# Routing the second of four token batches one step sooner, and re-laying the last attention step, in a fused attention and mixture-of-experts kernel

## The chip, the cores and the metric

The kernel runs on one core of a Trainium2 chip. The metric is the device time of one execution in microseconds. A program is executed several times; the median of the runs shown is compared, and one further execution is recorded by the hardware profiler. TensorE (PE) multiplies matrices, VectorE (DVE) and ScalarE (ACT) work on rows of 128 partitions, GpSimd (POOL) does small arithmetic and issues gathers and scatters, and SyncE (SP) issues the plain transfers. Each engine runs its own list of instructions in order, and the lists wait for each other through semaphores.

## The reference

Attention with a local window of 96 keys and 8 global keys over 4 batches of 768 tokens and 8 heads, then a mixture of 8 experts in which every token goes to the one expert with the largest logit:

```python
scores = scale * q @ k.T + bias            # masked to 8 global and 96 local keys
a = softmax(scores);  x = (a @ v)          # 3072 tokens x 512
logits = x @ w_gate + modality_bias[modality_id]
e_idx = np.argmax(logits, axis=1)
gate_w = softmax(logits)[np.arange(N), e_idx]
for e in range(E):
    mask = e_idx == e
    h = np.maximum(x[mask] @ w1[e], 0.0)
    out[mask] = gate_w[mask, None] * (h @ w2[e])
```

## The kernel before

**Attention.** The 3072 tokens are 24 blocks of 128, six to a batch. `step(n)` for n = 0 to 24 is a software pipeline. In step n PE computes the scores of block n (`s_mm`, tiles `s`), DVE adds the bias and finds the maxima (`red`, tiles `sc` and `nmx`), ACT takes the exponentials (`pr`). For block n-1 PE turns the exponentials (`t_mm`, tiles `pt`), and DVE or ACT copies them out (`t_cp`, tiles `pT`: of the three, the first by DVE, two by ACT). For block n-2 PE multiplies with the values (`pv`, tiles `x`), DVE divides (`rinv`, `xr`) and turns the rows for the gate (`xt`), and SP writes them to `x_rows` in DRAM. Step 24 has no block of its own: it finishes blocks 22 and 23.

**Routing.** Two steps after a batch is complete its logits are made (`gate_b`, `gate_c`: steps 8, 14, 20 for batches 0, 1, 2). The functions `route_m` (DVE finds the maximum `mx`, POOL makes `dl` and `cand`), `route_o` (DVE reduces `cand` to `cm`, POOL makes the one-hot `oh`), `route_e`, `route_b` (PE counts with a triangular matrix into `pk`, DVE copies it to `pks`, POOL adds up `base` and `pos`), `route_d`, `route_f` and `route_c` (POOL scatters a row for each token into `ids_sorted`) are put behind later steps by `at(step, function, ...)`; `after(n)` runs them at the end of step n. `route_o` is called inside the step, between `rinv` and `xr`, through the table `mids`.

**The first experts.** From the counts of batches 0 and 1 POOL makes a plan (`plan_parts`, four pieces, tiles `uei`, `uoi`, `inv`): two slots `e0` and `e1` of 512 tokens of one expert each. SP loads the weights of `e0` (`ld_first`, tile `raw`) and the token lists (`ld_lists`, tile `ui`; for `e1` also `ld_q`, tile `uq`), POOL gathers the rows of `e0` (`gather_x`, tile `xg`, four pieces of 128 rows), PE turns them (`x_pe`, tiles `mt`), ACT and DVE split them into a rounded part `xh` and a remainder `xl` (`x_lo`). The weights are split likewise (`split`, `split_lo`: `ah` and `al`). Then the slots run: `l1` (first product, tile `ph`, then `hh` by ACT and `hl` by DVE) and `l2` (second product, tile `po`), 512-column matmuls from there to the end.

**What sets the order.** PE, ACT and DVE run in the order in which the code is written. The order of POOL and SP is chosen by a scheduler from the same program. PSUM has eight banks: `p_p` has two (`pt`), `p_x` two (`x`, later `ph`), `p_t` four (`s`, `mt` and others); a tile waits until the last reader of the bank's former tile is done.

Of the kernel before, what the change touches and what calls it, by code (L numbers as in the profile page):

```python
# [9 lines left out]
F32 = mybir.dt.float32  # L10
F32R = mybir.dt.float32r
# [58 lines left out]
def moe_attention_kernel(  # L70
# [16 lines left out]
    def p_t(name):  # L87
        return psum.tile([P, 512], F32, tag="pR", name=name, bufs=4)
# [342 lines left out]
    def gate_c(b):  # L431
        lgts[b] = gp.tile([P, NB, E], F32, tag="lgt", name=f"lgt{b}")
        lps = gt.pop(b)
        lq = p_t(f"lq{b}")
        for u in range(NB // 2):
            nc.tensor.matmul(
                lq[:, 2 * E * u : 2 * E * u + 2 * E], lps[:, u * P : (u + 1) * P], sel, start=True, stop=True
            )
        V.tensor_add(
            lgts[b],  # L440
            lq[:, 0 : NB * E].rearrange("p (t e) -> p t e", e=E),
            tbias[:, b * NB : (b + 1) * NB, :],
        )
# [72 lines left out]
    def route_b(b):  # L516


        oh = rt.pop(b)
        pk = (p_t if b + 1 < B else p_p)(f"pk{b}")  # L520
        ohf = oh.rearrange("p a e -> p (a e)")
        nc.tensor.matmul(pk[:, 0 : NB * E], tri, ohf, start=True, stop=True)
        nc.tensor.matmul(pk[:, NB * E : 2 * NB * E], ones, ohf, start=True, stop=True)
        pks = gp.tile([P, 2 * NB * E], F32, tag="pks", name=f"pks{b}", bufs=1)
        V.tensor_copy(pks, pk[:, 0 : 2 * NB * E])
        eng = nc.gpsimd if b + 1 < B else V
        for j in range(NB):
            eng.tensor_add(base[:, b, j + 1, :], base[:, b, j, :], pks[:, (NB + j) * E : (NB + j + 1) * E])
        if b + 1 < B:
            eng.tensor_copy(base[:, b + 1, 0, :], base[:, b, NB, :])  # L530
        pos = t3(b, "pos")
        eng.tensor_tensor(pos, pks[:, 0 : NB * E].rearrange("p (a e) -> p a e", e=E), base[:, b, 0:NB, :], ALU.add)
        eng.tensor_tensor(pos, pos, bm(ebase, NB), ALU.add)
        eng.tensor_tensor(pos, pos, oh, ALU.mult)
        rt[b, "pos"] = pos
# [141 lines left out]
    def ld_q(s):  # L677
        n = P * s.nt
        so = nc.sync.value_load(s.o_src, min_val=0, max_val=E * NT)
        s.uq = idq.tile([P, 4, 4, IDW], I32, tag="uq", name=f"uq{s.name}")  # L680
        src = ids[ds(so, n), :].rearrange("(g i t) o -> i g (t o)", g=4, t=s.nt)
        for b in range(4):
            nc.sync.dma_start(
                s.uq[M * b : M * b + M].rearrange("p g t o -> p g (t o)")[:, :, 0 : s.nt * IDW], src
            )
# [101 lines left out]
    def x_lo(s, t):  # L787
        sl = slice(t * P, (t + 1) * P)
        V.tensor_tensor(s.xl[:, :, sl], s.xf.pop(t), s.xh[:, :, sl].bitcast(F32), ALU.subtract)
# [7 lines left out]
        return s.hi[which, h, c // 2], s.lo[which, h, c // 2], c % 2 * 512  # L797

    def l1(s, g, bank=p_x):

        ph = bank(f"ph{s.name}{g}")
        nt = s.nt
        hh = mp.tile([P, 512], F32R, tag="hh", name=f"hh{s.name}{g}", bufs=3)
        hl = mp.tile([P, 512], F32R, tag="hl", name=f"hl{s.name}{g}", bufs=3)
        s.h[g] = hh, hl
        if nt == 1:
            for c in range(4):
                hi, lo, o = both(s, "a", g, c)
                xh, xl = s.xh[:, c, 0:P], s.xl[:, c, 0:P]
                nc.tensor.matmul(ph, xh, hi[:, o : o + 512], start=(c == 0), stop=False)  # L810
                nc.tensor.matmul(ph, xh, lo[:, o : o + 512], start=False, stop=False)
                pe_end[0] = nc.tensor.matmul(ph, xl, hi[:, o : o + 512], start=False, stop=(c == 3))
            s.ph = ph
            s.hr = mp.tile([P, 512], F32, tag="hr", name=f"hr{s.name}{g}")
            last[0] = nc.scalar.activation(s.hr, ph, AF.Relu)
            return
        n, k = P * nt, 4 // nt
        for i in range(k):
            f = k * g + i
            fs = f % 4 * P  # L820
            for c in range(4):
                hi, lo, o = both(s, "a", f // 4, c)
                hi, lo = hi[:, o + fs : o + fs + P], lo[:, o + fs : o + fs + P]
                xh, xl = s.xh[:, c, 0:n], s.xl[:, c, 0:n]
                out_ = ph[:, i * n : (i + 1) * n]
                nc.tensor.matmul(out_, hi, xh, start=(c == 0), stop=False)  # L826
                nc.tensor.matmul(out_, hi, xl, start=False, stop=False)  # L827
                pe_end[0] = nc.tensor.matmul(out_, lo, xh, start=False, stop=(c == 3))  # L828
        last[0] = nc.scalar.activation(hh, ph, AF.Relu)  # L829
        V.scalar_tensor_tensor(hl, ph, 0.0, hh.bitcast(F32), ALU.max, ALU.subtract)  # L830

# [311 lines left out]
    def at(n, f, *args):  # L1143
        todo.setdefault(n, []).append((f, args))
# [139 lines left out]

    LAST = NBLK - NB
    for b in range(B):
        n0 = b * NB
        eng = nc.gpsimd if b + 1 < B else V
        at(n0 + NB + 3, route_m if b + 1 < B else route_a, b)
        if b + 1 < B:  # L1290
            mids[n0 + NB + 4] = b
        at(n0 + NB + 4, route_e, b)
        at(n0 + NB + 4, route_b, b)
        at(n0 + NB + 5, route_d, b, eng)
        if b + 1 < B:
            at(n0 + NB + 6, route_f, b)
        if b + 2 == B:
            for g in range(4):
                at(n0 + NB + 6, lambda g=g: gather_q(eslots[1], 0, g, pt_end))
        for j in range(NB):  # L1300
            at(n0 + NB + 6 + (j, j // 3, j // 2, j // 2)[b], write_in_step, b, j)
# [73 lines left out]
            next(plan_e, None)  # L1375

    for j in range(4):
        at(LAST - 1 + j, plan_part)

    def pool(name, bufs=1):  # L1380
        return sM.enter_context(tc.tile_pool(name=name, bufs=bufs, side="right", reuse_waits="tile"))
# [17 lines left out]
    def ld_lists():  # L1399
        with tc.issue_after(v_last[0].ins):  # L1400
            for s in eslots:
                lists[0] = ld_x(s)
                if not s.rows:
                    ld_q(s)


    def first_lo(j, h):
        fs = slice(512 * h, 512 * h + 512)
# [7 lines left out]
    at(LAST + 1, open_moe)  # L1416
    for j in range(2):
        at(LAST + 3, ld_first, "a", j)
    at(LAST + 4, ld_lists)
    at(LAST + 4, lambda: load_v(NBLK - 1, lists[0]))  # L1420
    for t in range(4):
        at(LAST + 4, lambda t=t: gather_x(eslots[0], t, pt_end if t > 1 else pv_end))
    for n, j, h in ((3, 0, 0), (4, 0, 1), (5, 1, 0)):
        at(LAST + n, split, None, "a", 0, j, h)
        los[LAST + n + 1] = j, h
# [16 lines left out]
    def step(n):  # L1442

        on, back = n < NBLK, 0 < n <= NBLK
        if n + 2 < NBLK:
            load_q(n + 2)
            load_k(n + 2)
        if n < VE:
            load_v(n)
        if VE - 2 < n < NBLK - 2:  # L1450
            load_v(n + 1)
        if n == 1:
            consts_l()
        if on:
            s_mm(n, 0)
            s_mm(n, 1)
        if n == 1:

            for j in range(NP):
                if j < 3:  # L1460
                    for hh in HEADS[(0, 4, 6)[j] : (4, 6, 8)[j]]:
                        red(n, hh)
                if j in (0, 2):
                    t_mm(0, j)
                    t_cp(0, j, j == 2)
            return after(n)
        if on:
            for hh in HEADS[0:6]:
                red(n, hh)
        if n > 1:  # L1470
            pv(n - 2)
        if n > NB and n % NB == 2:
            gate_b(n // NB - 1)
        if on:
            for hh in HEADS[6:H]:
                red(n, hh)
        if n in los:
            first_lo(*los[n])
        if not on:
            x_pe(eslots[0], 0, p_t)  # L1480
            x_pe(eslots[0], 1, p_t)
        if n > 1:
            rinv(n - 2)
        if n in mids:
            route_o(mids[n])
        if back:
            t_mm(n - 1, 0)
            t_mm(n - 1, 1)
        if n > 1:
            xr(n - 2)  # L1490
        if back:
            t_cp(n - 1, 0)
            t_cp(n - 1, 1, True)
        if n > 1:
            xt(n - 2)
        if not on:
            x_lo(eslots[0], 0)
            x_lo(eslots[0], 1)
        if not on:
            x_t(eslots[0], 2, p_t)  # L1500
        if back:
            t_mm(n - 1, 2, p_t)
            t_cp(n - 1, 2, True)
        if not on:
            x_t(eslots[0], 3, p_t)
            split(eslots[0], "a", 0, 1, 1)
            first_lo(1, 1)
        if n > NB and n % NB == 2:
            gate_c(n // NB - 1)
        after(n)  # L1510

    def after(n):

# [12 lines left out]
    pv(NBLK - 1)  # L1526
    sQ.close()
    mp = pool("mp")
    xr(NBLK - 1)
    l1(e0, 0, p_t)  # L1530
    xt(NBLK - 1)
    split(e0, "b", 0, 0)
    l1(e0, 1)
# [357 lines left out]
```

## Time and profile before

| | |
|---|---|
| median of 3 runs | 411.37 us (408.71 to 838.96) |
| profiled execution | 408.98 us |
| its span, first to last instruction | 407.2 us |
| mean granted TensorE clock | 0.998 of full speed |
| PE busy | 391.6 us, 96% |
| DVE, ACT, POOL busy | 267.5, 228.9, 190.7 us |
| steps 21, 22, 23 begin on PE (scores of the block) | 105.98, 110.29, 115.95 us |
| first matmul of the experts | 129.34 us |

Times in the trace are microseconds from the start of the span. A row of the timeline gives the start, the duration, engine, line, operation, the tile written and those read, how many instructions of that form stand together, and in brackets how long the engine had been idle before it and what released it. "Busy" of PE counts modelled ends of pipelined matmuls, so a busy PE is not a measure of speed; the idle times in brackets are what counts.

### The profile page before, as it was taken

The page shows a single profiled execution, that of the slowest core. Times are in us where ns is not written, and L with a number is a line of the kernel's source. Part 1 is how long each engine was busy: PE and PEld are TensorE (multiplying, and loading weights), DVE is VectorE, ACT ScalarE, POOL GpSimd, SP SyncE. Part 2 cuts the span into 40 slices and gives each one's busy share as a digit, 9 for nine tenths or more (in the row PEclk, how much of TensorE's full clock was granted, in tenths as well). Part 3 has the DMA queues.
Part 4 walks back from the last instruction along what each step waited for, and adds up shares of the span by engine and source line. Part 5 has one row for each costly group of instructions (what it writes and reads, how often), then busy time and mean ns, then how long its engine had stood idle before and what let it go on. Part 6 is the DMA issues. An engine that isn't in the chain of part 4 may idle for free.

```text
span 407.2 us, 10964 instructions
## 1 busy us (share of the span) xinstructions
PE 391.6 (96%) x3900; PEld 326.9 (80%) x3900; DVE 267.5 (66%) x859; ACT 228.9 (56%) x609; POOL 190.7 (47%) x334
## 2 busy tenths in 40 slices
PE   8889999999989999999999999999999999999993
PEld 7678888888778788888878888888888888888992
DVE  7889899899897598989455344486444775543220
ACT  7988898898893543362335333396233784233511
POOL 7700042167877777138786767223777240000301
PEclk9999999999999999999999999999999999999999
DMA  8999999999848953313925654369745389210201
GB/s 243 324 351 321 303 320 291 301 301 326 300 136 282 314 192 120 108 58 103 328 55 191 234 185 147 131 212 326 246 158 156 129 265 333 87 59 2 104 2 58
DMA packets 47536, 82.49 MB, mean 203 GB/s; under 512 B 11296, under 2 KB 24480, under 8 KB 47473
## 3 DMA queue, kind: packets, MB, share of 16 engines
q1 hardware_dynamic: 41296, 68.68, 51.6%
q0 software_dynamic: 5632, 12.76, 9.2%
q8 instruction: 33, 0.54, 0.5%
q10 hardware_dynamic: 544, 0.26, 0.2%
q14 instruction: 31, 0.25, 0.2%
HBM read 68.19 MB, written 13.55 MB: 201 GB/s over the span
## 4 chain that ended last, share of the span: by engine, by line
PE 83%; ACT 7%; issue 5%; DVE 2%; POOL 1%; POOLq 0%; DVEq 0%
ACT pr L316 6%; PE s L285 6%; PE pt L337 5%; PE php L826 5%; PE php L827 5%; PE php L828 5%; PE pop L856 5%; PE pop L854 5%; PE pop L855 5%; PE x L376 5%; PE phe L826 4%; PE poe L854 4%; PE phe L828 4%; PE phe L827 4%; PE poe L856 4%
## 5 line engine op out<-in xcount | busy, mean ns | idle before, releaser
L316 ACT ACTIVATE pr<-sc,nmx 128x168 f32<-128x168 f32 (+1 forms) x192 | 79.7, 417 | 10.8 <-DVE nmx L305 10.5
L830 DVE SCALAR_TENSOR_TENSOR hlp<-php,hhp 128x512 fp32r<-128x512 f32 x24 | 16.6, 692 | 64.5 <-ACT hhp L829 64.5
L716 POOL DMA_INDIRECT xgp<-x_rows,iqp x48 | 51.4, 1071 | 15.2 <-issue 11.6
L829 ACT ACTIVATE hhp<-php 128x512 fp32r<-128x512 f32 x24 | 14.4, 598 | 75.3 <-PE php L828 75.3
L305 DVE CUSTOM_DVE_ANT_0 sc<-s,tbl 128x168 f32<-128x168 f32 (+1 forms) x192 | 49.9, 321 | 7.1 <-PE s L285 4.8
L954 POOL DMA_INDIRECT out<-obp,oip x12 | 14.0, 1168 | 65.2 <-ACT obp L953 62.7
L285 PE MATMUL s<-kb,qt 64*64 64x168 f32 (+1 forms) x768 | 40.4, 314 | 3.5 <-ACT pT L345 2.6
L826 PE MATMUL php<-xhp,ahp 128*128 128x512 f32 x96 | 37.8, 393 | 0.0
L285 PEld LDWEIGHTS s<-kb,qt 64*64 64x64 f32 x768 | 28.3, 136 | 11.8 <-ACT pT L345 5.7
L827 PE MATMUL php<-xlp,ahp 128*128 128x512 f32 x96 | 37.4, 390 | 0.0
L828 PE MATMUL php<-xhp,alp 128*128 128x512 f32 x96 | 37.4, 390 | 0.0
L854 PE MATMUL pop<-bhp,hhp 128*128 128x512 f32 x96 | 37.4, 389 | 0.0
L855 PE MATMUL pop<-blp,hhp 128*128 128x512 f32 x96 | 37.4, 389 | 0.0
L856 PE MATMUL pop<-bhp,hlp 128*128 128x512 f32 x96 | 37.4, 389 | 0.0
L316 ACT ACTIVATION_READ_ACCUMULATOR pr<-sc,nmx 128x1 f32 x192 | 36.0, 188 | 0.0
L337 PE MATMUL pt<-ident,pr 128*128 128x128 f32 x272 | 35.1, 278 | 0.0
L559 POOL DMA_INDIRECT ids_sorted<-tki,pi x24 | 24.3, 1012 | 21.9 <-PE x L376 8.9
L337 PEld LDWEIGHTS pt<-ident,pr 128*128 128x128 f32 x272 | 29.4, 141 | 3.5 <-issue 1.9
L376 PE MATMUL x<-vx,pT 128*64 128x64 f32 x768 | 28.3, 225 | 1.7 <-issue 1.0
L829 ACT ACTIVATE hhe<-phe 128x512 fp32r<-128x512 f32 x16 | 9.6, 598 | 33.9 <-PE phe L828 33.8
L376 PEld LDWEIGHTS x<-vx,pT 128*64 128x64 f32 x768 | 24.6, 137 | 4.8 <-issue 1.4
L826 PE MATMUL phe<-xhe,ahe 128*128 128x512 f32 x64 | 25.3, 395 | 0.0
(392 smaller groups left out, 974.0 us busy)
## 6 DMA issues: line engine op xcount, KB each, us to landing
vx<-in_v_l SPq DMA_DIRECT2D x20, 512.0 KB
x_rows<-xr SPq DMA_DIRECT2D x48, 128.0 KB
qt<-in_q_t SPq DMA_DIRECT2D x23, 256.0 KB
kb<-in_k_t SPq DMA_DIRECT2D x6, 816.0 KB
vl<-in_v_s SPq DMA_DIRECT2D x20, 160.0 KB
rawe0a<-in_moe_w SPq DMA_DIRECT2D x4, 512.0 KB
rawe0b<-in_w SPq DMA_DIRECT2D x4, 512.0 KB
rawe1a<-in_w SPq DMA_DIRECT2D x4, 512.0 KB
```

The costliest lines, as they stand in the source:

```text
L285: nc.tensor.matmul(ps[h][64 * H2 : 64 * H2 + 64, s * W : s * W + w], qt[hs, hp, 64 * s : 64 * s + 64], kt[hs, hp, k0 : k0 + w], start=True ...
L305: V.tensor_tensor_reduce(out=sc, in0=pss[n, hp // 2][h][:, hp % 2 * W : hp % 2 * W + w], in1=(tbl0 if starts(n) else tbl)[:, hh, :], op0=A ...
L316: last[0] = nc.scalar.activation(pr[:, h * (PRW - W) : h * (PRW - W) + w], sc, AF.Exp, bias=nmx[:, hh : hh + 1], scale=-1.0, accum_out=sum ...
L337: pt_end[0] = nc.tensor.transpose(tp[:, i * P : (i + 1) * P], pr[:, o : o + P], ident)
L376: pv_end[0] = nc.tensor.matmul(px[h][64 * H2 : 64 * H2 + 64, o : o + D], pT[:, 64 * H2 : 64 * H2 + 64], vx[:, 0 if first else s, (2 * hp + ...
L716: ins = nc.gpsimd.indirect_dma_start(out=s.xg[:, t, g * P : (g + 1) * P], out_offset=None, in_=s.xsrc.rearrange("n (b d) -> (n b) d", b=4) ...
L826: nc.tensor.matmul(out_, hi, xh, start=(c == 0), stop=False)
L827: nc.tensor.matmul(out_, hi, xl, start=False, stop=False)
L828: pe_end[0] = nc.tensor.matmul(out_, lo, xh, start=False, stop=(c == 3))
L854: nc.tensor.matmul(s.po[t], hh[:, tt], hi, start=(fc == 0), stop=False)
L855: nc.tensor.matmul(s.po[t], hh[:, tt], lo, start=False, stop=False)
L856: pe_end[0] = nc.tensor.matmul(s.po[t], hl[:, tt], hi, start=False, stop=(fc == 7))
```

## The change

- `gate_c` and `route_b` of all batches take their PSUM bank from `p_p` in place of `p_t`.
- Everything that routes batch 1 (`route_m` to `route_c`) comes one step sooner, and the plan pieces too (steps 16 to 19 in place of 17 to 20). Of batch 2 `route_b` and `route_d` come one step later (23 and 24); its `route_m`, `route_o` and `route_e` stay.
- The lists are loaded, and the four gathers of `e0` issued, behind step 21 in place of 22; `ld_q` of `e1` is put behind the load of the last values.
- Step 24 is written out anew as `finish`: all four `x_pe` first, then `pv(22)`, the turns of block 23 (its third copy now by DVE, the first by ACT), and the first group of matmuls of `l1` before `pv(23)`; its copies out (`l1_out`) follow behind `pv(23)`.

```diff
@@ gate_c, route_b
-        lq = p_t(f"lq{b}")
+        lq = p_p(f"lq{b}")
...
-        pk = (p_t if b + 1 < B else p_p)(f"pk{b}")
+        pk = p_p(f"pk{b}")
@@ l1
-    def l1(s, g, bank=p_x):
-
-        ph = bank(f"ph{s.name}{g}")
+    def l1(s, g, bank=p_x):
+        l1_mm(s, g, bank)
+        l1_out(s, g)
+
+    def l1_mm(s, g, bank):
+
+        ph = s.ph = bank(f"ph{s.name}{g}")
...
+    def l1_out(s, g):
...
@@ the table of steps
-        n0 = b * NB
+        n0 = b * NB - (b + 1 == BE)
         eng = nc.gpsimd if b + 1 < B else V
         at(n0 + NB + 3, route_m if b + 1 < B else route_a, b)
         if b + 1 < B:
             mids[n0 + NB + 4] = b
         at(n0 + NB + 4, route_e, b)
-        at(n0 + NB + 4, route_b, b)
-        at(n0 + NB + 5, route_d, b, eng)
+        late = b + 2 == B
+        at(n0 + NB + 4 + late, route_b, b)
+        at(n0 + NB + 5 + late, route_d, b, eng)
...
-        at(LAST - 1 + j, plan_part)
+        at(LAST - 2 + j, plan_part)
...
-    at(LAST + 4, ld_lists)
+    at(LAST + 3, ld_lists)
     at(LAST + 4, lambda: load_v(NBLK - 1, lists[0]))
+    at(LAST + 4, ld_quarters)
     for t in range(4):
-        at(LAST + 4, lambda t=t: gather_x(eslots[0], t, pt_end if t > 1 else pv_end))
+        at(LAST + 3, lambda t=t: gather_x(eslots[0], t, pt_end))
@@ step
+        if not on:
+            return finish(n)
...
+    def finish(n):
+
+        e0 = eslots[0]
+        first_lo(*los[n])
+        for t in range(4):
+            x_pe(e0, t, p_t)
+        x_lo(e0, 0)
+        x_lo(e0, 1)
+        pv(n - 2)
+        rinv(n - 2)
+        split(e0, "a", 0, 1, 1)
+        t_mm(n - 1, 0)
+        t_mm(n - 1, 1)
+        x_lo(e0, 2)
+        x_lo(e0, 3)
+        t_cp(n - 1, 0, True)
+        t_cp(n - 1, 1, True)
+        xr(n - 2)
+        t_mm(n - 1, 2)
+        first_lo(1, 1)
+        t_cp(n - 1, 2)
+        after(n)
+        l1_mm(e0, 0, p_t)
+        xt(n - 2)
@@ behind the steps
     pv(NBLK - 1)
     sQ.close()
     mp = pool("mp")
+    l1_out(e0, 0)
     xr(NBLK - 1)
-    l1(e0, 0, p_t)
     xt(NBLK - 1)
```

The scheduler's order on POOL between the plan's last instruction and the counts of batch 2 (steps 21 and 22) was this; `xge<-x_rows,uie` are the gathers of `e0`, `dl`, `cand`, `ne`, `oh` belong to batch 2, `ale` is half of a weight's remainder:

```order
L1363 TENSOR_SCALAR inve<-inve 128x8
L485 TENSOR_TENSOR dl_2870<-lgt_2728,mx_2868 128x48
L487 TENSOR_SCALAR cand_2872<-dl_2870 128x48
L757 TENSOR_TENSOR ale_2889<-rawe0a_2884,ahe_2888 128x512
L488 TENSOR_TENSOR cand_2872<-cand_2872,erev 128x48
L498 TENSOR_TENSOR ne_2977<-erev,cm_2975 128x48
L500 TENSOR_SCALAR oh_2979<-ne_2977 128x48
L690 DMA xge_3065<-x_rows,uie_3035 128x512 x4
```

It is now, at the same place of POOL's list:

```order
L1373 TENSOR_SCALAR inve<-inve 128x8
L485 TENSOR_TENSOR dl_2870<-lgt_2747,mx_2868 128x48
L690 DMA xge_2910<-x_rows,uie_2897 128x512 x4
L487 TENSOR_SCALAR cand_2872<-dl_2870 128x48
L757 TENSOR_TENSOR ale_2916<-rawe0a_2884,ahe_2915 128x512
L488 TENSOR_TENSOR cand_2872<-cand_2872,erev 128x48
L498 TENSOR_TENSOR ne_3004<-erev,cm_3002 128x48
L500 TENSOR_SCALAR oh_3006<-ne_3004 128x48
```

The four gathers moved from behind `oh` to between `dl` and `cand`.

On DVE the reduction of that `cand` stands in the same place in both programs, in step 22 between `rinv` and `xr`; the copy `pks` moved a step back. It was:

```order
L391 RECIPROCAL rin_2972<-rin_2972 128x8
L496 TENSOR_REDUCE cm_2975<-cand_2872 128x6
L398 TENSOR_TENSOR xr_2991<-x_0_2931,rin_2972 128x4x64
L398 TENSOR_TENSOR xr_2991<-x_1_2932,rin_2972 128x4x64
L347 COPY pT_0_2996<-pt_0_2981 128x512
L416 STREAM_TRANSPOSE xT_2719<-xr_2991 128x2x8x32
L525 COPY pks_3013<-pk_3010 128x96
L305 ISA sc_0_3093,nmx_3092<-s_0_0_3071,tbl 128x168
```

It is now, at the same place of DVE's list:

```order
L391 RECIPROCAL rin_2999<-rin_2999 128x8
L496 TENSOR_REDUCE cm_3002<-cand_2872 128x6
L398 TENSOR_TENSOR xr_3018<-x_0_2958,rin_2999 128x4x64
L398 TENSOR_TENSOR xr_3018<-x_1_2959,rin_2999 128x4x64
L347 COPY pT_0_3023<-pt_0_3008 128x512
L416 STREAM_TRANSPOSE xT_2738<-xr_3018 128x2x8x32
L305 ISA sc_0_3077,nmx_3076<-s_0_0_3055,tbl 128x168
```

Only `pks` left this stretch; `cm` still stands ahead of the copy `pT` and of the next block's `sc`.

On PE in step 24, from the turns of the gathered rows (`mt`) to the products of block 23 (`x` from `vl`), the order was:

```order
L782 MATMUL mte_3233<-ident,xge_3065 128x128 x4
L782 MATMUL mte_3239<-ident,xge_3065 128x128 x4
L337 MATMUL pt_0_3248<-ident,pr_162 128x128 x3
L337 MATMUL pt_0_3248<-ident,pr_163 128x128
L337 MATMUL pt_1_3253<-ident,pr_163 128x128 x2
L337 MATMUL pt_1_3253<-ident,pr_164 128x128 x2
L782 MATMUL mte_3270<-ident,xge_3065 128x128 x4
L337 MATMUL pt_2_3277<-ident,pr_164 128x128
L337 MATMUL pt_2_3277<-ident,pr_165 128x128 x3
L782 MATMUL mte_3284<-ident,xge_3065 128x128 x4
L364 MATMUL x_0_3310<-vl_79,pT_0_3263 64x64
```

On PE from the end of step 23 (turns of block 22, then batch 2's counts `pk`) to the products of block 22 (`x` from `vl`), it is now:

```order
L337 MATMUL pt_2_3159<-ident,pr_160 128x128
L337 MATMUL pt_2_3159<-ident,pr_161 128x128 x3
L522 LDWEIGHTS tri
L522 MATMUL pk_3166<-oh_3006,tri 128x48
L523 LDWEIGHTS ones
L523 MATMUL pk_3166<-oh_3006,ones 128x48
L782 MATMUL mte_3188<-ident,xge_2910 128x128 x4
L782 MATMUL mte_3194<-ident,xge_2910 128x128 x4
L782 MATMUL mte_3200<-ident,xge_2910 128x128 x4
L782 MATMUL mte_3206<-ident,xge_2910 128x128 x4
L364 MATMUL x_0_3214<-vl_78,pT_0_3154 64x64
```

All sixteen turns now stand ahead of the products of block 22, behind `pk`; `pk` takes the bank that `pt_0` of block 22 had.

## Rows read from the trace of the kernel before

**Rows 1.** The page: the chain that ended last, shares by engine

```profile
PE 83%; ACT 7%; issue 5%; DVE 2%; POOL 1%; POOLq 0%; DVEq 0%
```

**Rows 2.** PE's waits in the whole span: total, times, longest (first and last of ten)

```profile
PE s L285 <- ACT pT L345: 2.6, 5, 1.2
...
PE pk L522 <- POOL oh L500: 0.2, 1, 0.2
```

**Rows 3.** Timeline of PE, steps 21 to 24

```profile
105.98 1.37 PE L285 MATMUL s<-kb,qt 64*64 64x168 f32 x32
...
110.29 1.06 PE L285 MATMUL s<-kb,qt 64*64 64x168 f32 x18
...
121.82 0.69 PE L364 MATMUL x<-vl,pT 64*64 64x64 f32 x32 [0.88 <-DVE pT L347]
...
123.53 1.09 PE L782 MATMUL mte<-ident,xge 128*128 128x128 f32 x8
124.46 1.04 PE L337 MATMUL pt<-ident,pr 128*128 128x128 f32 x8
125.33 0.60 PE L782 MATMUL mte<-ident,xge 128*128 128x128 f32 x4
...
127.08 0.63 PE L782 MATMUL mte<-ident,xge 128*128 128x128 f32 x4 [0.71 <-PE pt L337]
127.64 0.69 PE L364 MATMUL x<-vl,pT 64*64 64x64 f32 x32
```

**Rows 4.** Timeline of DVE, steps 21 to 23

```profile
111.44 0.16 DVE L483 TENSOR_REDUCE mx<-lgt 128x6 f32<-128x48 f32 x1
...
113.75 0.80 DVE L390 TENSOR_SCALAR rin<-sums 128x8 f32<-128x8 f32 x1
...
114.79 0.20 DVE L496 TENSOR_REDUCE cm<-cand 128x6 f32<-128x48 f32 x1
114.97 0.76 DVE L398 TENSOR_TENSOR xr<-x,rin 128x256 f32<-128x256 f32 x2
...
116.86 0.22 DVE L525 COPY pks<-pk 128x96 f32<-128x96 f32 x1
117.00 0.32 DVE L305 CUSTOM_DVE_ANT_0 sc<-s,tbl 128x168 f32<-128x168 f32 x1
...
121.08 0.68 DVE L347 COPY pT<-pt 128x512 f32<-128x512 f32 x1
```

**Rows 5.** Timeline of ACT between steps 22 and 23

```profile
116.60 0.62 ACT L751 CAST ahe<-rawe0a 128x512 fp32r<-128x512 f32 x1
117.37 0.43 ACT L316 ACTIVATE pr<-sc,nmx 128x168 f32<-128x168 f32 x1
```

**Rows 6.** Timeline of POOL, steps 21 to 23

```profile
111.58 0.19 POOL L1357 CAST uoie<-uofe 128x2 int32<-128x2 f32 x1
...
112.58 0.26 POOL L485 TENSOR_TENSOR dl<-lgt,mx 128x48 f32<-128x48 f32 x1
112.93 0.34 POOL L487 TENSOR_SCALAR cand<-dl 128x48 f32<-128x48 f32 x1
...
114.47 0.29 POOL L488 TENSOR_TENSOR cand<-cand,erev 128x48 f32<-128x48 f32 x1
...
116.48 1.10 POOL L690 DMA_INDIRECT xge<-x_rows,uie  x1 [0.72 <-PE pk L523]
...
120.39 0.95 POOL L690 DMA_INDIRECT xge<-x_rows,uie  x1 [0.30 <-issue]
121.37 0.21 POOL L528 TENSOR_TENSOR base<-base,pks 128x8 f32<-128x8 f32 x1
```

**Rows 7.** Timeline of SP's queue: scores' input of block 23, and the two lists

```profile
105.17 0.41 SPq L145 DMA_DIRECT2D qt<-in_q_t  x1
...
112.86 1.50 SPq L674 DMA_DIRECT2D uie<-ids_sorted  x2
```

**Rows 8.** Line 690, the gathers: from issue to landing

```profile
DMA to landing us min/median/max: 5.3/5.3/5.3
```

More of the change, by code (lines that the diff above doesn't have):

```diff
@@ L799, in l1 @@
     def l1(s, g, bank=p_x):
-        ph = bank(f"ph{s.name}{g}")
+        l1_mm(s, g, bank)
+        l1_out(s, g)
+    def l1_mm(s, g, bank):
+        ph = s.ph = bank(f"ph{s.name}{g}")
         nt = s.nt
-        hh = mp.tile([P, 512], F32R, tag="hh", name=f"hh{s.name}{g}", bufs=3)
-        hl = mp.tile([P, 512], F32R, tag="hl", name=f"hl{s.name}{g}", bufs=3)
-        s.h[g] = hh, hl
         if nt == 1:
@@ L812, in l1 @@
                 pe_end[0] = nc.tensor.matmul(ph, xl, hi[:, o : o + 512], start=False, stop=(c == 3))
-            s.ph = ph
-            s.hr = mp.tile([P, 512], F32, tag="hr", name=f"hr{s.name}{g}")
-            last[0] = nc.scalar.activation(s.hr, ph, AF.Relu)
             return
@@ L828, in l1 @@
                 pe_end[0] = nc.tensor.matmul(out_, lo, xh, start=False, stop=(c == 3))
+    def l1_out(s, g):
+        ph = s.ph
+        hh = mp.tile([P, 512], F32R, tag="hh", name=f"hh{s.name}{g}", bufs=3)
+        hl = mp.tile([P, 512], F32R, tag="hl", name=f"hl{s.name}{g}", bufs=3)
+        s.h[g] = hh, hl
+        if s.nt == 1:
+            s.hr = mp.tile([P, 512], F32, tag="hr", name=f"hr{s.name}{g}")
+            last[0] = nc.scalar.activation(s.hr, ph, AF.Relu)
+            return
         last[0] = nc.scalar.activation(hh, ph, AF.Relu)
@@ L1402, in ld_lists, with ld_quarters @@
                 lists[0] = ld_x(s)
-                if not s.rows:
-                    ld_q(s)
+    def ld_quarters():
+        with tc.issue_after(v_last[0].ins):
+            ld_q(eslots[1])
     def first_lo(j, h):
@@ L1478, in step @@
             first_lo(*los[n])
-        if not on:
-            x_pe(eslots[0], 0, p_t)
-            x_pe(eslots[0], 1, p_t)
         if n > 1:
@@ L1495, in step @@
             xt(n - 2)
[L1496 to L1500, printed above, removed]
         if back:
@@ L1503, in step @@
             t_cp(n - 1, 2, True)
[L1504 to L1507, printed above, removed]
         if n > NB and n % NB == 2:
```

## The prediction

> **What bounds the kernel now.** I read the chain that ended last first: 83% of it is PE [rows 1]. The list of PE's waits has ten entries, from 2.6 us down to 0.2 us [rows 2]; their releasers are all of the attention part or its routing, and none is a product of the experts. From 129.34 us, where the first expert matmul starts, PE runs without a wait to its last products. So the end of the span moves by what the start of the expert products moves, plus or minus PE work placed on the other side of it. An edit in the attention steps counts only as far as it changes that start.
>
> In the steps themselves three engines run almost level. Step 21 takes 4.3 us on PE (105.98 to 110.29) [rows 3]. Between steps 22 and 23 ACT ends a cast at 117.22 and begins the next exponential at 117.37, held only until DVE delivers the first `sc` at 117.00 to 117.33 [rows 4, 5]. There is 0.15 us of slack between DVE and ACT there, so a delay of DVE in step 22 goes almost whole into step 23. In step 24 PE loses 0.88 us waiting for DVE's copy `pT` and 0.71 us before the last group of turned rows [rows 3]; that last wait is for the fourth gather, issued at 120.39 and landed 5.3 us after its issue at the nearest [rows 6, 8]. These 1.6 us are all that a better step 24 could take from PE's waits.
>
> **Banks.** No instruction is added. `lq` and `pk` now wait for the bank of the first `pt`, which DVE empties in the same step. In step 22 the counts would have waited until that copy; but there they go away with the later `route_b`. For the other batches I take 0, with bounds of 0.3 us each way per batch: PE loses 0.2 us at `pk` at worst now [rows 2], and the copy that it would wait for starts within a step's last microsecond.
>
> **Batch 1 a step sooner, and the lists.** The same POOL work moves forward by one step, 4.3 us. The plan's address `uoi` was ready at 111.77, and SP issued the first list at 112.86 [rows 6, 7]. Both come 4.3 to 4.5 us sooner: list at about 108.4. From its issue to the first gather there were 3.6 us, at the end of which POOL had been idle for 0.72 us [rows 6, 7], so I take 3.6 us as the upper bound of a list's landing: 112.0 us. SP's queue is moved too: the input `qt` of block 23, issued at 105.17 before, now stands behind the two lists, at about 110. Its scores run some 6 us later, and that covers it; were it late, DVE's delay below would still hide some 4 us.
>
> **The gathers ahead of `cand`.** This is the term that decides. POOL now has `dl`, four gathers, then `cand`, the weight half `ale`, and `cand` again. `dl` needs `mx`, which DVE makes at 111.44 to 111.60 at the end of step 21 [rows 4]; `dl` takes 0.26 us, so the gathers can start at 112.05, just when the list has landed. The four took from 116.48 to 121.34, 4.86 us, at 0.95 to 1.10 us each with 0.30 us between [rows 6]. That POOL's arithmetic waits behind them is in the rows: `base` needed `pks`, ready at 117.08, and started at 121.37, 0.03 us behind the last gather [rows 4, 6]. So `cand` begins at about 116.94, and from its start to its end are 1.83 us (112.93 to 114.76, with `ale` between) [rows 6]: it ends at 118.8. DVE stands at `cm` from 114.79 [rows 4], in step 22, with `xr`, the copy `pT` and all of step 23's `sc` queued behind it. It waits 4.0 us. `pks` leaves this stretch, which gives 0.14 us back (116.86 to 117.00) [rows 4]. The first `sc` of step 23 thus starts at 120.9 in place of 117.0: 3.9 us late. ACT, with its 0.15 us of slack, follows; PE has the scores done and waits for `pT` and then the exponentials.
>
> One rule bears on the price of these gathers. In step 22 DVE's `rin`, a small operation, took 0.80 us beside POOL's weight half [rows 4]; beside the gathers no gather took longer than 1.10 us [rows 6]. The Trainium skill, SBUF — State Buffer, section Who interferes with whom, says that DVE in a two-port mode and GpSimd exclude each other from a shared port, so that descriptors of GpSimd's transfers starve while DVE holds it. By it the gathers, now beside step 22's DVE work, could grow by the length of `rin`, and the sum by up to 0.8 us; the rows of the gathers show no such growth, and the sum goes without it.
>
> **Step 24 anew.** PE waits for the copy `pT` of block 22 as before (its products started at 121.82 behind it [rows 3]), now in front of `pk`, whose bank that copy frees: 121.82 + 3.9 = 125.7. By then all four gathers have landed (the last issued at about 116, plus 5.3 us [rows 8]), so the 0.71 us wait is gone. Then follow on PE: `pk`, 0.14 us (bounded by two matmuls of a tenth each); sixteen turns, twice 0.93 us (123.53 to 124.46) = 1.86; the products of block 22, 1.71 (121.82 to 123.53); eight turns of block 23, 0.87 (124.46 to 125.33); and four more, 0.44, which now share a bank with the first four and wait for ACT's copy of these, some 0.2 us [rows 3]. Sum 5.2 us: the expert products begin at 130.9. Before, PE was at the products of block 23 at 127.64 with the same work left [rows 3]; the two orders differ only in which of `pv(23)` and the first group of `l1` is first. So PE is 3.3 us late. One wait is new: the second group of `l1` takes a bank that `xr` of block 23 empties, and the first group no longer runs meanwhile. Half of the 0.76 us of an `xr` pair [rows 4] is 0.4 us. The copies that moved between ACT and DVE are covered: both engines end before PE needs them. Total 3.7 us.
>
> **The sum.** Profiled execution 408.98 us + 3.7 = 412.7 us (span 410.9). The profiled time is the better base than the median of 411.37, since the lowest run is 408.71; the median keeps 2.4 us of spread that the new runs may also show. So 0.9% slower.
>
> **Rivals.**
> *The wait at `cm` doesn't happen.* If the gathers did not hold POOL's arithmetic, `cand` would end by 115.3, the point below which DVE's and ACT's slack and the earlier landing make up for it. Then step 24's edits stand alone: 121.82 + 5.2 + 0.4 = 127.44 against 127.64, so 0.2 us faster; with 0.3 us from banks for each of three batches and some of the 0.71 us, up to 1.5 us. Time 407.5 to 408.8 us, not slower. For it speaks that a gather moves data on other hardware than POOL; against it the row of `base`. Chance 0.15.
>
> *The list lands late, and the wait is longer.* The list now follows a megabyte of weights and the last blocks' inputs in the transfer engines, where it had them to itself before. Every microsecond of landing past 112.0 delays the gathers, `cand` and DVE by as much. A landing at 114 to 116 gives 414.5 to 416.5 us. For it: the 3.6 us were measured with SP's queue stalled. Against it: SP issues the list some 4 us behind those loads. Chance 0.2.
>
> *The tail doesn't follow.* POOL's work for batch 2 and the gathers of `e1` come 4 us later as well; if a product of the experts then waits, 1 to 2 us are added: 414 to 415 us. Chance 0.05.
>
> **How the numbers follow.** The forecast, 410.5 to 414 us, has 0.6. The range 407.5 to 416.5 takes in the first rival's time, the late list up to a landing at 116, and the median's spread of 2.4 us on top of the forecast. A change of 2%, 8.2 us, is about what a measurement of this kernel tells from none. Slower by more needs a list later than 116, or several delays at once: 0.06. Faster by more would need more than all of PE's waits in the last steps: 0.02. Within 2%: 0.92.
>
> **What would show it.** DVE's `cm` of batch 2 begins at 118.8 with an idle time of 4 us, released by POOL's `cand`; the gathers start at 112.0; the first exponential of step 23 is at 121.3; no wait stands before the turns of the rows; the first expert product is at 130.9 and `pv(23)` behind it. The prediction is wrong if `cm` shows no idle time, or if the gathers start later than 113.

## The result, and the profile after

| | before | after |
|---|---|---|
| median | 411.56 us (4 runs, 408.71 to 838.96) | 416.57 us (4 runs, 414.36 to 417.57) |
| profiled execution, span | 408.98, 407.2 us | 417.49, 415.8 us |
| mean granted clock | 0.998 | 0.989 |

The changed kernel takes 1.0146 times as long, 95% interval 1.0102 to 1.0191: 6.0 us of 411 more, 4 to 8 by the interval. The ratio is taken from fast runs alone, which leaves out the one of 838.96 us. The direction was forecast, the size (3.7 us) was not; the median lies just above the range.

PE's waits in the changed kernel: who waited for whom, then total, number and longest.

```profile
PE x L364 <- DVE pT L347: 4.1, 1, 4.1
PE s L285 <- ACT pT L345: 2.0, 3, 1.2
PE x L376 <- issue: 1.8, 2, 1.5
PE x L364 <- issue: 1.2, 1, 1.2
...
PE phe L824 <- DVE xr L398: 0.4, 1, 0.4
```

Against [rows 2], a single wait of 4.1 us is new at the head of the list: PE stands, ahead of the products of block 21 in step 23, for a `pT` that DVE writes. The 0.4 us at `phe` is the forecast wait of the second group of expert products. The timeline of DVE says why `pT` is late.

```profile
113.73 0.16 DVE L483 TENSOR_REDUCE mx<-lgt 128x6 f32<-128x48 f32 x1
...
116.11 0.17 DVE L390 TENSOR_SCALAR rin<-sums 128x8 f32<-128x8 f32 x1
...
122.28 0.20 DVE L496 TENSOR_REDUCE cm<-cand 128x6 f32<-128x48 f32 x1 [5.78 <-POOL cand L488]
122.46 0.76 DVE L398 TENSOR_TENSOR xr<-x,rin 128x256 f32<-128x256 f32 x2
123.13 0.68 DVE L347 COPY pT<-pt 128x512 f32<-128x512 f32 x1
```

DVE stands 5.78 us at `cm`, where it had no idle time before [rows 4]. Since the whole profile is 2.29 us late at `mx` already (113.73 against 111.44), the delay is best read from `mx` to `cm`: 8.55 us, where it was 3.35 us [rows 4]. That is 5.2 us more. The idle time is larger than the delay because `rin` takes 0.17 us here and 0.80 before [rows 4].

The timeline of POOL has what DVE waits for.

```profile
113.97 0.27 POOL L485 TENSOR_TENSOR dl<-lgt,mx 128x48 f32<-128x48 f32 x1 [3.50 <-DVE mx L483]
115.53 1.09 POOL L690 DMA_INDIRECT xge<-x_rows,uie  x1 [1.29 <-PE s L285]
...
119.44 0.95 POOL L690 DMA_INDIRECT xge<-x_rows,uie  x1 [0.30 <-issue]
120.42 0.36 POOL L487 TENSOR_SCALAR cand<-dl 128x48 f32<-128x48 f32 x1
120.75 1.26 POOL L757 TENSOR_TENSOR ale<-rawe0a,ahe 128x512 fp32r<-128x512 f32 x1
121.97 0.28 POOL L488 TENSOR_TENSOR cand<-cand,erev 128x48 f32<-128x48 f32 x1
```

Four gathers and their issue gaps are 4.86 us, as in [rows 6], and `cand` begins 0.03 us behind the last, as `base` did there. But 1.29 us lie between the end of `dl` and the first gather, which the forecast had at nothing. The rows of POOL's sequencer (POOLq) have four waits for the gathers:

```profile
L690 POOLq EVENT_SEMAPHORE  x4: 17/43/43, 113.9 to 114.7; - x4
```

The last one begins 0.86 us ahead of the gather, as in the kernel before. The third waits for the list of `e0`: by the semaphore that the list's transfer raises, its last piece landed at 114.56, 0.32 us behind the end of `dl`. The experiment with the two lists exchanged (e17, below) comes back to this.

PE in steps 23 and 24:

```profile
118.01 1.76 PE L285 MATMUL s<-kb,qt 64*64 64x168 f32 x32
123.87 1.13 PE L364 MATMUL x<-vl,pT 64*64 64x64 f32 x32 [4.10 <-DVE pT L347]
124.93 1.97 PE L376 MATMUL x<-vx,pT 128*64 128x64 f32 x32
126.83 2.82 PE L337 MATMUL pt<-ident,pr 128*128 128x128 f32 x12
...
129.56 2.15 PE L782 MATMUL mte<-ident,xge 128*128 128x128 f32 x16
...
135.15 0.47 PE L824 MATMUL phe<-xhe,ahe 128*128 128x512 f32 x1
```

The sixteen turns run without a wait, as forecast, and the first expert product is at 135.15. Behind its stand PE runs slower: products of this form took 0.69 us at full clock [rows 3], and 1.13 here. A table by stretches (busy time of PE, PEld, DVE, ACT, POOL, then the granted clock, the share of the transfer engines and GB/s) has the clock:

```profile
120.00:123.00 3.00, 0.00 (x0) 0.00 (x0) 0.72 (x3) 0.00 (x0) 2.56 (x6) 1.00 0.96 265
123.00:130.00 7.00, 6.13 (x80) 5.83 (x81) 6.52 (x27) 4.30 (x18) 1.10 (x5) 0.51 0.68 210
130.00:133.00 3.00, 3.00 (x72) 2.76 (x72) 2.11 (x6) 3.00 (x7) 2.42 (x10) 1.00 0.77 253
```

After PE stood for 4.1 us, the granted clock is at its lower level (1.2 GHz) for about 7 us.

What made the profile late before step 22 is in part PE waiting for its own instructions. First before, then after, the same instructions in steps 3 and 4, whose code is the same:

```profile
23.06 0.34 PE L364 MATMUL x<-vl,pT 64*64 64x64 f32 x7 [0.57 <-issue]
...
29.42 0.86 PE L376 MATMUL x<-vx,pT 128*64 128x64 f32 x22 [0.99 <-issue]
```

```profile
23.72 0.34 PE L364 MATMUL x<-vl,pT 64*64 64x64 f32 x7 [1.24 <-issue]
...
30.62 0.86 PE L376 MATMUL x<-vx,pT 128*64 128x64 f32 x22 [1.54 <-issue]
```

That is 1.2 us of the 2.29 which the change didn't make. A single profile carries such gaps, so below the delay is read between two points of one profile, and sizes are taken from the timed ratios.

### The profile page after: what moved, and what is told of

The parts are those of the page before. It is cut to its first block, busy times and chain, and to the rows that moved or that the text cites. A ratio compares the mean times of both kernels' runs of the same rounds, so it can differ in the third digit from the quotient of the medians.

```text
span 415.8 us, 10956 instructions
## 1 busy us (share of the span) xinstructions
PE 394.9 (95%) x3900; PEld 328.9 (79%) x3900; DVE 266.4 (64%) x859; ACT 228.7 (55%) x609; POOL 193.0 (46%) x334
## 4 chain that ended last, share of the span: by engine, by line
PE 76%; issue 7%; ACT 6%; DVE 4%; POOL 3%; DMA 2%; SPq 1%; POOLq 0%; DVEq 0%; ACTq 0%
PE pt L337 5%; PE php L824 5%; PE php L826 5%; PE s L285 5%; PE pop L865 5%; PE pop L863 5%; PE php L825 5%; PE pop L864 5%; ACT pr L316 5%; PE x L376 4%; PE phe L824 3%; PE poe L865 3%; PE phe L825 3%; PE phe L826 3%; PE poe L863 3%
## 5 line engine op out<-in xcount | busy, mean ns | idle before, releaser
L716 POOL DMA_INDIRECT xgp<-x_rows,iqp x48 | 50.3, 1048 | 15.1 <-issue 11.5
L337 PE MATMUL pt<-ident,pr 128*128 128x128 f32 x272 | 36.6, 284 | 0.3 <-ACT pT L345 0.3
L559 POOL DMA_INDIRECT ids_sorted<-tki,pi x24 | 26.6, 1108 | 16.3 <-PE s L285 6.8
L337 PEld LDWEIGHTS pt<-ident,pr 128*128 128x128 f32 x272 | 30.4, 144 | 4.2 <-issue 1.9
L376 PE MATMUL x<-vx,pT 128*64 128x64 f32 x768 | 29.2, 229 | 2.6 <-issue 1.8
```

The costliest lines, as they stand in the source:

```text
L337: pt_end[0] = nc.tensor.transpose(tp[:, i * P : (i + 1) * P], pr[:, o : o + P], ident)
L376: pv_end[0] = nc.tensor.matmul(px[h][64 * H2 : 64 * H2 + 64, o : o + D], pT[:, 64 * H2 : 64 * H2 + 64], vx[:, 0 if first else s, (2 * hp + ...
L716: ins = nc.gpsimd.indirect_dma_start(out=s.xg[:, t, g * P : (g + 1) * P], out_offset=None, in_=s.xsrc.rearrange("n (b d) -> (n b) d", b=4) ...
```

## Experiments

My theory: the wait at `cm` behind the gathers carries the loss. The rivals: the banks of `lq` and `pk` carry it (the profile is late before the gathers); the new last step carries it; the lower clock behind PE's stand is what makes the wait dear. All ratios are to the kernel before on the same chip.

**Gathers behind `cand` (e1).** The changed kernel with one edit, the gathers held until the second instruction of `cand`:

```diff
-        G.tensor_tensor(cand, cand, bm(erev, NB), ALU.mult)
+        rt[b, "cg"] = G.tensor_tensor(cand, cand, bm(erev, NB), ALU.mult)
...
+    def behind_cand(t):
+        with tc.issue_after(rt[2, "cg"].ins):
+            gather_x(eslots[0], t, pt_end)
...
-        at(LAST + 3, lambda t=t: gather_x(eslots[0], t, pt_end))
+        at(LAST + 3, behind_cand, t)
```

> The changed kernel, with the four gathers of e0 held until the second cand of batch 2. If the wait at cm is what the change loses (5.8 us in the changed kernel's trace, and with it the lower granted clock behind it): cm has under 0.5 us of idle time, and the time is 4 to 6 us below the changed kernel's 416.6, 410 to 412. If the banks or the last step carry the loss, cm's wait goes but the time stays at 414 to 416.

412.43 us, 1.0063 [1.0029, 1.0097].

```profile
114.89 0.15 DVE L496 TENSOR_REDUCE cm<-cand 128x6 f32<-128x48 f32 x1
```

`cm` has no idle time, and 3.4 us of the loss are gone (2.3 us either way, from the two intervals); 2.6 us stay. The wait looks like the larger part, not the whole.

**Banks alone (e2).** Before, with `lq` and `pk` on the bank tag of the turned probabilities:

```diff
-        lq = p_t(f"lq{b}")
+        lq = p_p(f"lq{b}")
...
-        pk = (p_t if b + 1 < B else p_p)(f"pk{b}")
+        pk = p_p(f"pk{b}")
```

> The kernel before, with the banks of lq and pk alone moved to the tag of the turned probabilities. The changed kernel was already 2.2 us late by step 14. If that is the banks (three batches, 0.07 us at lq and 0.15 us at pk visible), 412 to 414. If it is the spread of PE's issue gaps from run to run (0.67 and 0.55 us longer in steps 3 and 4, where the two programs are the same), within 0.5 us of the kernel before.

411.54 us, 1.0035 [1.0003, 1.0068], between the two. Its profile has an issue gap of 1.81 us at 30 us, so it can't say more; e18 asks again.

**The changed kernel with the old last step (e3), and before with the new last step alone (e4).** `finish()` and the split of `l1` are taken out of the one and put into the other.

> The changed kernel with the last step's code as before (banks, batch 1 sooner, lists and gathers sooner kept). If the wait at cm carries the loss, it is there again, about 5 us, and the time is 414 to 418. If the new last step carries it, 410 to 412.

> The kernel before with the new last step alone. The turns of all four rows now stand ahead of the products of block 22, and the last gathers land no sooner than before (issued 120.4, 5.3 us): PE waits for the third and fourth at 124 to 126 us with those products behind it. If so 1 to 2.5 us slower than before, 410 to 412 by the profiled 409. If the order of the last step gains by itself, 0.2 to 1 us faster.

e3: 415.48 us, 1.0131 [1.0096, 1.0165], with 5.46 us of idle time at `cm`; so the loss doesn't need the new last step. e4: 415.49 us, 1.0129 [1.0091, 1.0167], more than twice what I expected. Its list of PE's waits begins:

```profile
PE mte L782 <- DMA xge<-x_rows,uie: 4.7, 4, 2.1
```

With the rows landing as late as before, each of the four turns waits for its gather, and the products of block 22 stand behind all four. The new last step thus needs the early gathers, and the changed kernel has both.

**Cand first with the old banks (e7), and the schedule alone (e8).** e7 is e1 with the two bank lines undone. e8 undoes the last step too: what is left is batch 1 a step sooner, `route_b` of batch 2 a step later, lists and gathers sooner, `cand` ahead of the gathers.

> The changed kernel with cand ahead of the gathers and with the banks of lq and pk as before; the new last step stays. If the banks cost 0.8 us by step 22, as the trace of the cand-first kernel has it against before, 0.6 to 1 us below that kernel's: ratio 1.003 to 1.005. If the banks cost nothing, 1.006.

> The kernel before with batch 1 a step sooner, its lists and gathers sooner and cand ahead of the gathers; banks and last step as before. The rows land sooner, so the 0.71 us that PE waited ahead of the last turned rows goes: ratio 0.997 to 1.000. If the new last step were what gains, this would be at 1.005 or more.

e7: 411.08 us, 1.0017 [0.9982, 1.0053]. e8: 409.62 us, 0.9998 [0.9967, 1.0029]. The earlier schedule by itself costs and gives nothing that can be measured; the 0.7 us ahead of the last turned rows, which I expected to go, are still there in e8, though its last gather was issued at 119.69:

```profile
128.25 0.63 PE L782 MATMUL mte<-ident,xge 128*128 128x128 f32 x4 [0.71 <-PE pt L337]
```

It is the same 0.71 us with the same releaser as before [rows 3], so the rows don't set it.

**The gathers put back into e8 (e9, again as e13).**

```diff
-        at(LAST + 3, behind_cand, t)
+        at(LAST + 3, behind_dl, t)
+    at(LAST + 3, cand_late, 2)
```

`behind_dl` holds the gathers until `dl`, `cand_late` makes `cand` behind the last gather (their code is left out here).

> The schedule-only kernel (0.9998 of before) with one thing put back: POOL issues the four gathers between dl and cand of batch 2, as in the changed kernel; banks and last step are as before. If the wait at cm alone carries the greater part of the loss: 5 to 6 us of idle time at cm, and a ratio of 1.009 to 1.013 (3.5 to 5.5 us). If it needs the new banks and the new last step to cost that much, below 1.005.

> The gathers-ahead kernel again, since PE's issue gaps filled the other session. As there: if the wait at cm alone carries the greater part of the loss, 5 to 6 us of idle time at cm and a ratio of 1.009 to 1.013 to before; if it needs the new banks and last step to cost that much, below 1.005.

e9 to e12 ran while PE's instructions came late on that chip, for the kernel before too (440.29 us in place of 410); their ratios (0.9989, 1.0007, 0.9994 and 0.9874, intervals of 0.9% to 1.4%) say nothing of the change. PE's waits of e9 begin:

```profile
PE x L376 <- issue: 4.8, 10, 1.1
PE x L364 <- issue: 4.3, 9, 1.1
```

The four were run again. e13: 415.93 us, 1.0133 [1.0082, 1.0185]. Its DVE and POOL:

```profile
112.72 0.16 DVE L483 TENSOR_REDUCE mx<-lgt 128x6 f32<-128x48 f32 x1
...
121.30 0.20 DVE L505 TENSOR_REDUCE cm<-cand 128x6 f32<-128x48 f32 x1 [5.79 <-POOL cand L494]
```

```profile
112.97 0.27 POOL L485 TENSOR_TENSOR dl<-lgt,mx 128x48 f32<-128x48 f32 x1 [4.00 <-DVE mx L483]
114.55 1.09 POOL L699 DMA_INDIRECT xge<-x_rows,uie  x1 [1.32 <-PE s L285]
```

From `mx` to `cm` are 8.58 us, as in the changed kernel. e8 and e13 differ on POOL in the place of the four gathers alone (SP's queue, ordered by the scheduler, has one pair of writes of `x_rows` a few places later in e13): 1.35%, 5.5 us. That is nearly all of the 6.0 us, though the two intervals leave 2.5 us either way. Their profiles agree: from `mx` to the first expert product are 23.38 us in e13 (to 136.10) and 17.38 us in e8 (113.13 to 130.51).

**Two gathers ahead of `cand`, two behind (e6).** In `behind_cand`, `t < 2` goes without the wait.

> The changed kernel with two gathers of e0 ahead of cand of batch 2 and two behind it: half the dose. If the wait at cm is the gathers, each 1.25 us on POOL, it falls from 5.8 to about 3.3 us, and the time by 1.5 to 2.5 us, between the changed kernel and the one with cand first (1.0063). If the wait is the list's landing alone, cm's wait and the time stay within 1 us of the changed kernel's.

412.18 us, 1.0052 [1.0020, 1.0084].

```profile
117.54 0.20 DVE L496 TENSOR_REDUCE cm<-cand 128x6 f32<-128x48 f32 x1 [2.96 <-POOL cand L488]
```

The idle time is as expected for half the dose, the time isn't: it is that of e1, with no wait at all. With the new banks and last step the first 2.5 us of delay at `cm` (5.86 us from `mx`, against 3.35) cost nothing that can be measured beside e1, which stands elsewhere: 1.65 us at `pk` and 0.93 us for the rows. From there to the changed kernel's delay are 2.7 us more, and they cost 3.9 us, 2.3 us either way.

**The lower clock (e5, e11, e15).** 40 matmuls for PE while it stands: the second half of block 23's scores, five times over, into the same banks.

```diff
+        if n == NBLK - 1:
+            for _ in range(5):
+                s_fill(n)
```

In e5 this stands behind the first six `red()` of the step, in e11 and e15 ahead of them; `s_fill` itself is left out here.

> The changed kernel with 40 matmuls more in step 23, ahead of the products of block 21: they compute the second half of that block's scores five times again, into the same banks, while PE would stand 4.1 us. In the changed kernel's trace the granted clock is 0.5 from 123.4 to 130.0 us, behind that stand. If that level carries part of the loss, the clock stays at 1.00 and the time falls by 1.5 to 2.5 us, to 414 or 415. If DVE and not PE sets the pace behind the wait (cm to the first expert product takes 12.87 us, and 12.85 before), the clock rises and the time stays within 0.7 us.

> The changed kernel with the 40 matmuls of the other filler run, now ahead of DVE's reads of these scores in the program, so that PE has them while DVE stands at cm. If the low granted clock behind PE's stand carries part of the loss, the clock stays at 1.00 and the time falls by 1.5 to 2.5 us to 414 or 415. If DVE sets the pace behind the wait, the clock rises and the time stays within 0.7 us of 416.6 (1.0146).

> The early-filler kernel again. With PE on time the 40 matmuls end by 122.8 us, ahead of the pT that PE waits for at 123.9. If the low granted clock behind the stand carries part of the loss: clock 1.00, and 1.5 to 2.5 us below the changed kernel (1.0146), at 1.008 to 1.011. If DVE sets the pace: clock 1.00 and 1.013 to 1.016.

e5 missed its aim: 421.66 us, 1.0298 [1.0243, 1.0352]. Behind `red` the matmuls write banks that DVE has still to read, so they waited 6.0 us for it and stood in front of the products. e15: 415.13 us, 1.0138 [1.0085, 1.0192], mean clock 0.998. PE:

```profile
121.98 0.69 PE L381 MATMUL x<-vl,pT 64*64 64x64 f32 x32 [1.06 <-DVE pT L364]
...
126.97 0.20 PE L539 MATMUL pk<-oh,tri 128*128 128x48 bf16 x1 [1.75 <-DVE pT L364]
...
132.41 0.48 PE L841 MATMUL phe<-xhe,ahe 128*128 128x512 f32 x1
```

The products run at 0.69 us, but PE then stands 1.75 us at `pk` for DVE. From `cm` (120.39) to the first expert product are 12.02 us, 12.87 in the changed kernel. So by these two profiles the lower clock is worth 0.85 us there; in the ratios it is 0.3 us, which is not resolved. For the most part DVE sets the pace.

**POOL's `ale` ahead of the gathers (e10, e14).** In e1, POOL's and DVE's `ale` fell together:

```profile
119.40 1.60 DVE L757 TENSOR_TENSOR ale<-rawe0a,ahe 128x512 fp32r<-128x512 f32 x1
```

```profile
119.14 1.30 POOL L757 TENSOR_TENSOR ale<-rawe0a,ahe 128x512 fp32r<-128x512 f32 x1
```

```diff
-        with tc.issue_after(rt[2, "cg"].ins):
+        with tc.issue_after(rt[2, "al"].ins):
...
-        at(LAST + 3, behind_cand, t)
+        at(LAST + 4, behind_cand, t)
```

`rt[2, "al"]` is POOL's `ale`, itself behind `cand`.

> The cand-first kernel (1.0063) with POOL's weight half ale ahead of the gathers too. In the cand-first trace POOL's ale ran from 119.14 to 120.44 and DVE's ale beside it took 1.60 us in place of 0.69. If these two hold each other up, DVE's ale takes 0.7 us here and the ratio falls by 0.002 to 1.004. If DVE's long ale has another cause, it stays at 1.6 us and 1.006. POOL's ale will then lie beside DVE's rin or xr of step 22.

> The ale-first kernel again. Banks and last step as in the changed kernel, no wait at cm, DVE's ale at 0.69 us as in its other trace: a ratio of 1.003 to 1.005 if the two ale held each other up for 0.9 us in the cand-first kernel (1.0063), 1.006 if that cost nothing.

Apart from POOL's, DVE's `ale` takes 0.69 us in e10 and in e14, so the two held each other up. The time didn't follow: e14 413.46 us, 1.0082 [1.0049, 1.0116]. Its profile has PE waiting for the rows, for longer than the 0.93 us of e1:

```profile
PE mte L782 <- DMA xge<-x_rows,uie: 1.5, 1, 1.5
```

Behind that stand the products of block 22 take 1.13 us, and 0.69 in e1. Whether this takes the gain back is not shown, as the ratios of e1 and e14 don't differ beyond their intervals.

**Banks in e8 (e18).** e18 is e8 with the new banks and, so that the two `ale` don't fall together, with POOL's `ale` ahead of the gathers as in e14.

> The schedule-only kernel (0.9998) with the new banks of lq and pk, and POOL's ale ahead of the gathers so that it doesn't lie beside DVE's: banks alone, without a wait at cm and with the old last step. If the banks cost 1 to 2 us, as the banks-only kernel has it (1.0035, interval 1.0003 to 1.0068): 1.003 to 1.005. If they cost nothing and the new last step made the loss of the cand-first kernels: 0.999 to 1.001.

409.98 us, 1.0009 [0.9987, 1.0032]. The banks by themselves are nothing that can be measured, and so is the new last step by itself with early rows (e7, 1.0017). Together, without the wait at `cm`, they were 1.0063 and 1.0082 (e1, e14); why the pair costs more than the two is not settled. The profiles point at `pk`: with the new banks it waits for the copy `pT`, and in the new last step the turns stand behind it (1.65 us in e1); with the old banks (e7) `pk` has no wait, and the first turns run while DVE copies. No run has this alone.

**The list of `e0` second (e17).** What holds the first gather for 1.1 to 1.3 us behind `dl`?

```diff
-            for s in eslots:
+            for s in reversed(eslots):
                 lists[0] = ld_x(s)
```

> The changed kernel with SP issuing the list of e1 first and that of e0 behind it, 1.1 us later. If the first gather waits for its list to land, as read from 4.7 us between issue and gather with the transfer engines 98% busy: the idle time of POOL between dl and the first gather grows from 1.3 to about 2.4 us, the wait at cm from 5.8 to about 6.9, and the time by 0.5 to 1.5 us over the changed kernel's 1.0146. If something else holds the first gather, nothing moves: 1.3 us, 5.8 us, 1.0146.

416.37 us, 1.0160 [1.0124, 1.0196]; `cm` stands 5.47 us.

```profile
116.46 0.27 POOL L485 TENSOR_TENSOR dl<-lgt,mx 128x48 f32<-128x48 f32 x1 [3.86 <-DVE mx L483]
117.82 1.09 POOL L690 DMA_INDIRECT xge<-x_rows,uie  x1 [1.10 <-PE s L285]
```

The list of `e0` went 1.2 us behind the other and the gather didn't move: it starts 1.36 us behind the start of `dl`, as in e3 and e6 (1.56 to 1.58 in the changed kernel and e13). The semaphores' times in the traces say why the run can't decide it: in e17 that list landed at 115.84, ahead of `dl`, as both lists did in e3 and e6. In the changed kernel and in e13 it landed behind the end of `dl` (114.56 against 114.24, 113.58 against 113.24), POOL's third wait was over 0.02 us later, and the gather is 0.2 us later than in the other three. So 0.2 us of the 1.29 are the list's landing. The other 1.09 us are there with the lists landed, and 0.86 of them lie between the beginning of POOL's last wait and the gather's start; why these take so long stays open.

**The turns of two rows ahead of block 22's products (e12, e16).** In e8, `x_pe(e0, 0)` and `x_pe(e0, 1)` go ahead of `pv(n - 2)`.

> The schedule-only kernel with the turns of the first two rows of e0 ahead of the products of block 22, where PE stood 0.69 us for a pT. The rows land by 122 (gathers from 115.78, 4 to 6 us), so that stand is filled: 0.3 to 0.7 us below schedule-only, ratio 0.998 to 0.999. If the rows land later than that, PE waits for them and it is 0.5 us or more slower.

> The turns-first kernel again. In its other trace PE's stand ahead of the products of block 22 was 0.53 us and lay behind the eight turns, but 0.93 us came ahead of the last turns, so the gain is what the earlier copies of the rows give: 0.3 to 0.7 us below schedule-only, 0.998 to 0.999; if the later wait takes it all back, 0.9998.

e16: 409.63 us, 0.9983 [0.9951, 1.0015]. The stand that it fills is gone, but no version here is measurably faster than the kernel before.

## Why the prediction was wrong

*What bounds the kernel.* Right: the delay at `cm` went through to the first expert product and to the end.

*Banks, taken as 0.* Borne out with the old last step (e18, 1.0009); `pk` waits 0.5 and 0.7 us there, and the time doesn't show it.

*Batch 1 a step sooner, lists, `qt` behind them.* Right: e8 has all of it at 0.9998, and no score waited for `qt`.

*The gathers ahead of `cand`.* This is the step that failed, in size. The place, the order on POOL, the 4.86 us of the gathers and the 1.83 us of `cand` and `ale` were right (4.86 and 1.83 again). The term said that the gathers start when `dl` ends, since I read the 0.72 us of POOL's idle time ahead of the first gather [rows 6] as the end of the list's landing. For the most part it is a gap that the first gather has also with the lists landed (1.09 us in e3, e6 and e17): 1.29 us here. On the time scale of the kernel before, 2.29 us earlier, the gathers started at 113.24, past the 113 that the prediction names as a sign of being wrong. Delay at `cm`: 4.0 forecast, 5.2 measured. Its price, 3.9 us forecast, is 5.5 us by e8 and e13, 2.5 us either way.

*Step 24 anew, -0.2 us, and 0.4 us at the second group.* The 0.4 us are there. The 0.71 us ahead of the last turned rows, which I put down to the fourth gather, were not that: they stay with earlier rows (e8). The changed kernel's order has no such wait all the same. From `cm` to the first expert product I had 12.1 us; e15, at full clock, has 12.02, the changed kernel 12.87 behind its lower clock, a term that I didn't have. On top of the wait at `cm`, banks and last step together are 1.0146 against 1.0133 (e13), 0.5 us, not resolved.

*The sum.* 3.7 us, and 6.0 measured (4 to 8). By the profile, the delay at `cm` is 1.2 us more than forecast, and the way from there to the first expert product 0.8 us more; with these two the forecast's own sum is 5.7 us. The ratios resolve neither of the two. The time, 416.57 us, lies 3.9 us above 412.7: 2.3 are this size, and 1.6 the base, the profiled 408.98 us which is one of the lower runs.

*Rivals.* That the wait doesn't happen fell at once. The late list had the right sign and price, 1:1 in the start of the gathers, but the list landed at 112.3 on the time scale of the kernel before, not at 114 to 116, and it holds the gathers for 0.2 us of the 1.29. The tail followed: 0.2 us at the last products of the first slot is all that is new there.

*The rule on the shared port.* The Trainium skill, SBUF — State Buffer, section Who interferes with whom, says that a DVE instruction with two SBUF inputs contends with a GpSimd instruction that reads SBUF. The trace agrees for the two `ale`: 1.60 us together, 0.69 apart. The gathers, beside DVE's steps, stayed at 0.95 us each, so the 0.8 us that I weighed for them didn't come.

## What to carry to other kernels

Before a transfer is issued earlier from an engine that also computes, look at what is queued behind it on that engine and who waits for that: here four gathers of 1.25 us each stood in front of a 0.3 us instruction on which DVE, ACT and PE hung in turn. An idle time ahead of an instruction is not yet a landing time: the times of the transfer's semaphore in the trace tell which it is, and a run that moves the transfer tells it only if the landing then comes late enough to matter. A delay has no fixed price: the first 2.5 us at `cm` cost nothing measurable where PE stood for other things, and the next 2.7 us cost about 4.

## What the runs showed that I had not expected

Behind 4.1 us of standing PE's granted clock was 0.51 from 123 to 130 us (changed kernel), and behind 1.81 us of waiting for instructions 0.58 from 30 to 32 us (e2), yet filling the first of these stands gained nothing measurable. PE's issue gaps in steps 3 and 4, whose code is the same, differ by 1.2 us in sum between two profiles, and in one stretch of runs made every kernel 30 us slower, before included. POOL stands 0.7 to 1.3 us ahead of the first indirect gather when a short instruction precedes it, and 0.16 us behind `cand` and `ale` (e7, e8); ahead of the following ones it stands 0.30 us. With the short instruction the gather starts 0.86 us behind the beginning of POOL's last wait, to the hundredth, in the kernel before, the changed one, e1, e3, e6, e13 and e17; in e7 and e8 it is 1.49 us, and the arithmetic lies within it.
